# Loads held back by GpSimd reads, a first MLP step in halves, and list-scheduler ranks found by a search: windowed attention with a rational MLP on one core

## The chip, the cores and the metric

One core of a Trainium2 chip runs the whole program. The metric is the device time of one execution in microseconds. Before: 273.1 us, median of three runs (272.65 to 273.63).

Names used below: PE is TensorE's matmuls, PEld its weight loads, DVE VectorE, ACT ScalarE, POOL GpSimd, SP SyncE. A "filler" is a matmul of the identity whose result nobody reads.

## The reference, cut to what matters

```python
def _attn_ref(q, k, v, n_sink, window):          # B 4, H 8, S 768, D 64; n_sink 4, window 128
    scores = scale * np.matmul(q, k.transpose(0, 1, 3, 2))
    keep = is_sink | in_window                   # the first 4 keys, and the last 128
    scores = np.where(keep, scores, -1000000000.0)
    ...                                          # softmax over the kept keys
    return np.matmul(a, v).astype(np.float32)

def _moe_ref(x, w_in, w_out, a, b):              # 3072 tokens, 512 -> 2048 -> 512
    h = x @ w_in
    P = a[0] + a[1] * h + a[2] * h2 + a[3] * h3
    Q = 1.0 + np.abs(b[0]) * np.abs(h) + np.abs(b[1]) * h2
    g = P / (Q + 1e-06)
    return (g @ w_out).astype(np.float32)
```

The attention output of all heads, put side by side, is the x of the MLP.

## The kernel before

The 3072 tokens are cut into 12 steps of 256. A step loads K, Q and V (GpSimd, float32 to bf16), transposes K and Q (from step 3 on by DMA, from SyncE), computes scores, exponentials and the weighted sum, writes a normalized `x_n`, transposes it into `xblk` (two halves, by DMA from SyncE from step 3 on), and then runs the MLP: first products, the rational function on ScalarE and VectorE, second products, store. Attention runs some two steps ahead of the MLP.

The program is not written in order. Every piece of work is registered with an engine, an assumed length, a rank and the pieces it must follow:

```python
for s in range(NSTEP):
    r_ = 4 * s - 20
    ...
            piece(("load_k", s, t), "POOL", 0.9, r_, lambda s=s, t=t: load_k(s, t),
                  [("turned_k", s - 2)] if s > 2 else [], kind="sw", load=0.88)
    ...
    for h in range(H):
        piece(("load_v", s, h), "POOL", 0.62, r_ + 1.0, lambda s=s, h=h: load_v(s, h),
              [("attend", s - 2, 2)] if s >= 3 else [("ones", s)], kind="sw", load=0.32)
...
                piece(("turn_k", s, t), "SP", 1.25, 4 * s - 14, ...
                piece(("placed_x", s, grp), "SP", 1.25, r_, lambda s=s, grp=grp: turn_x_half(s, grp),
                      norms + [free], kind="hw", load=0.8)
```

A list scheduler then plays this through with the assumed lengths: whenever an engine is free it takes, among the pieces whose predecessors are done in the plan, the one of lowest rank (now and then it leaves the engine idle for a piece of much lower rank that is about to be ready). The order in which pieces are taken is the order of each engine's queue. Where TensorE has nothing to do in the plan, fillers are put in that are meant to keep its clock up:

```python
w = min(able, key=lambda w_: (w_.rank, w_.order))
...
if spin_from <= now and free["PE"] <= now + 1e-9:
    n = int((then - now) / 0.056)
    ...
    w.run = lambda n=n: spin(n)
```

Each queue runs in order, so a piece that waits holds up all behind it (the wait of 4.2 us in the table below is one).

The softmax here doesn't subtract the row's maximum and nothing guards it: scores larger than these inputs give would overflow.

## Time and profile before

| | before |
|---|---|
| median time | 273.1 us |
| span of the profiled execution | 270.1 us |
| busy: PE, DVE, ACT, POOL | 247.4, 230.3, 224.3, 121.3 us |
| fillers in the program | 395 |
| length of the kernel's own plan | 256.9 us |
| landing of a transpose of x, median: 60 to 130 us, 130 to 240 us | 6.4 us, 2.5 us |
| longest wait of PE for a transpose of x | 4.2 us |

PE's busy time contains the fillers, so it overstates useful work. The length of the plan is what the list scheduler's assumed lengths add up to; it is no chip time. The lines themselves are in the prediction, which shows them.

### The profile page before, as it was taken

Reading aid. Unit: us, or ns where it says so; the run is one execution under the profiler, and the core shown is the slowest. Engines: PE = TensorE matmul, PEld = TensorE weight load, DVE = VectorE, ACT = ScalarE, POOL = GpSimd, SP = SyncE. Lnnn points to the kernel's source line nnn. Section 1 sums busy time; section 2 is a strip of 40 time slices with the busy share of each in tenths; the row PEclk is TensorE's granted clock in tenths of the full one; section 3 lists DMA queues with packets and bytes.
Section 4 is the critical chain, followed back from the end, with each engine's and each line's share of the span. In section 5 each row is a group of like instructions: output and inputs, shape, how many; then the busy total and the mean of one; then the engine's idle time right before and its main releaser. Section 6 shows DMA issues by size and latency. Waiting matters only on the chain.

```text
span 270.1 us, 5649 instructions
## 1 busy us (share of the span) xinstructions
PE 247.4 (92%) x2294; PEld 188.8 (70%) x2315; DVE 230.3 (85%) x293; ACT 224.3 (83%) x216; POOL 121.3 (45%) x178
## 2 busy tenths in 40 slices
PE   5899878898989759998989999999999999999994
PEld 4789777885776449877767777867858776665442
DVE  7975289869996398999998999999989999999950
ACT  8643758499979828799999999999999999899831
POOL 8955889879697496683925013280000000000000
PEclk9999999999999979999999999999999999999999
DMA  7999999999999999999996344491030211110222
GB/s 196 99 153 194 68 102 121 175 136 158 136 164 149 121 195 207 134 130 164 148 138 97 34 70 58 31 103 46 19 101 9 69 41 58 45 55 0 81 78 78
DMA packets 109674, 28.07 MB, mean 104 GB/s; under 512 B 101456, under 2 KB 105552, under 8 KB 109648
## 3 DMA queue, kind: packets, MB, share of 16 engines
q0 software_dynamic: 74288, 12.99, 73.0%
q1 hardware_dynamic: 35360, 14.72, 28.3%
q8 instruction: 18, 0.29, 0.5%
q14 instruction: 8, 0.07, 0.1%
HBM read 27.30 MB, written 6.29 MB: 124 GB/s over the span
## 4 chain that ended last, share of the span: by engine, by line
PE 53%; DMA 21%; POOL 10%; ACT 8%; SPq 3%; issue 3%; DVE 1%; ACTq 0%; POOLq 0%
PE ps_out L613 22%; PE ps_h L516 21%; DMA w_in_sb<-in_moe_w_in_dram 7%; DMA qT<-q_bf 5%; PE ps_o L468 5%; DMA q_bf<-in_q_dram 4%; POOL w_out_sb L188 3%; PE ps_s L414 3%; POOL v_bd L179 2%; DMA w_out_sb<-in_moe_w_out_dram 2%; DMA xblk<-x_n 2%; PE ps_s L373 2%; POOL k_bf L171 2%; SPq L318 2%; ACT lnq L577 1%
## 5 line engine op out<-in xcount | busy, mean ns | idle before, releaser
L516 PE MATMUL ps_h<-xblk,w_in_sb 128*128 128x256 bf16 x768 | 91.6, 275 | 4.6 <-DMA xblk<-x_n 4.2
L613 PE MATMUL ps_out<-w_out_sb,g 128*128 128x512 bf16 x363 | 86.8, 379 | 1.8 <-ACT o_t L618 0.6
L516 PEld LDWEIGHTS <-w_in_sb 128*128 128x128 bf16 x768 | 75.0, 99 | 17.9 <-issue 4.4
L179 POOL DMA_DIRECT2D v_bd<-in_v_dram x96 | 63.4, 682 | 44.0 <-PE ps_o L468 28.0
L613 PEld LDWEIGHTS <-g 128*128 128x128 bf16 x384 | 36.6, 98 | 37.0 <-issue 0.9
L523 ACT ACTIVATE hb<-ps_h 128x1024 bf16<-128x1024 f32 x48 | 49.7, 1042 | 13.0 <-PE ps_h L516 12.8
L577 ACT ACTIVATE lnq<-den,one_eps,qsc 128x2048 f32<-128x2048 bf16 x24 | 50.6, 2114 | 1.7 <-DVE den L551 1.6
L583 ACT ACTIVATE den<-lnq 128x2048 bf16<-128x2048 f32 x24 | 46.5, 1938 | 0.0
L432 ACT ACTIVATE e<-ps_s 128x768 bf16<-128x768 f32 x48 | 39.8, 834 | 7.0 <-PE ps_s L420 4.5
L373 PE MATMUL ps_s<-ident 128*128 128x128 bf16 x395 | 30.1, 226 | 6.9 <-ACT e L432 5.4
L551 DVE TENSOR_TENSOR den<-den,sq 128x2048 bf16<-128x2048 bf16 x24 | 29.1, 1221 | 3.1 <-ACT sq L538 2.8
L373 PEld LDWEIGHTS <-ident 128*128 128x128 bf16 x395 | 25.7, 102 | 8.3 <-issue 5.7
L468 PE MATMUL ps_o<-v_bd,e 128*128 128x130 bf16 x352 | 28.5, 219 | 0.1
L589 DVE TENSOR_TENSOR g<-num,den 128x4096 bf16<-128x4096 bf16 (+1 forms) x13 | 27.6, 2123 | 0.6 <-ACT den L583 0.5
L571 DVE TENSOR_TENSOR num<-num,sq 128x4096 bf16<-128x4096 bf16 (+1 forms) x13 | 27.6, 2122 | 0.1
L567 DVE TENSOR_TENSOR sq<-sq,hb 128x4096 bf16<-128x4096 bf16 (+1 forms) x13 | 27.6, 2121 | 0.1
L538 ACT ACTIVATE sq<-hb 128x2048 bf16<-128x2048 bf16 x14 | 27.1, 1936 | 0.1
L468 PEld LDWEIGHTS <-e 128*128 128x128 bf16 x352 | 24.5, 97 | 2.8 <-ACT e L432 0.2
L414 PE MATMUL ps_s<-qT,kT 128*128 128x192 bf16 x192 | 23.8, 246 | 1.6 <-DMA qT<-q_bf 1.0
L618 ACT ACTIVATE o_t<-ps_out 128x512 f32<-128x512 f32 x24 | 14.5, 614 | 11.7 <-PE ps_out L613 8.1
L171 POOL DMA_DIRECT2D k_bf<-in_k_dram x22 | 20.9, 961 | 5.5 <-DMA kT_flat<-k_bf 4.6
L155 POOL DMA_DIRECT2D q_bf<-in_q_dram x21 | 20.5, 984 | 5.6 <-DMA qT<-q_bf 3.1
(84 smaller groups left out, 238.4 us busy)
## 6 DMA issues: line engine op xcount, KB each, us to landing
out_dram<-o_t SPq DMA_DIRECT2D x24, 256.0 KB, 3.1
v_bd<-in_v_dram POOLq DMA_DIRECT2D x96, 32.0 KB, 4.8
k_bf<-in_k_dram POOLq DMA_DIRECT2D x22, 128.0 KB, 6.3
q_bf<-in_q_dram POOLq DMA_DIRECT2D x21, 128.0 KB, 6.3
w_in_sb<-in_moe_w_in_dram POOLq DMA_DIRECT2D x8, 256.0 KB, 8.8
w_out_sb<-in_moe_w_out_dram POOLq DMA_DIRECT2D x16, 128.0 KB, 4.7
stage_q<-in_q_dram SPq DMA_DIRECT2D x1, 768.0 KB, 6.5
stage_kv<-in_k_dram SPq DMA_DIRECT2D x1, 512.0 KB, 4.3
```

The lines of the kernel that those rows point to most:

```text
L179: nc.gpsimd.dma_start(out=v_bd[s][e * 64:(e + 1) * 64, i, :, e, 0:D], in_=v[b, h, g * TS:(g + 1) * TS, :].rearrange("(j p) d -> p j d", p=64))
L373: nc.tensor.matmul(ps_scores[:, 0, 384:384 + P], lhsT=ident, rhs=ident, start=True, stop=True)
L414: nc.tensor.matmul(ps[:, n // 2, (n % 2) * 192:(n % 2) * 192 + 192], lhsT=kT_fix[s % 2][:, i * NHF + n, :], rhs=qT_fix[b % 2][:, i, c:c + ...
L432: nc.scalar.activation(out=data.rearrange("p (a n) c -> p a n c", a=2), in_=ps[:, :, 0:384].rearrange("p a (n c) -> p a n c", n=2), func=A ...
L468: nc.tensor.matmul(ps_o[:, u - u0, :], lhsT=l_, rhs=r_.rearrange("p e c -> p (e c)"), start=(m == 0), stop=(m == len(terms) - 1))
L516: nc.tensor.matmul(ps[:, n, :], lhsT=w_in_sb[c][:, fc * P:(fc + 1) * P], rhs=xblk[m][:, c, :], start=(c == 0), stop=(c == NDMC - 1))
L523: nc.scalar.activation(out=hb[m][:, j * GW:(j + 1) * GW], in_=ps_h.pop((m, j)).rearrange("p n c -> p (n c)"), func=AF.Copy)
L551: nc.vector.tensor_tensor(out=den[m][:, c], in0=den[m][:, c], in1=sq[m][:, c], op=ALU.add)
L567: nc.vector.tensor_tensor(out=sq[m][:, c], in0=sq[m][:, c], in1=hb[m][:, c], op=ALU.mult)
L577: nc.scalar.activation(out=lnq[m, part], in_=den[m][:, c], func=AF.Ln, scale=qsc, bias=one_eps)
L583: nc.scalar.activation(out=den[m][:, c], in_=lnq[m, part], func=AF.Exp, scale=-1.0)
L613: nc.tensor.matmul(ps_out[m, tt], lhsT=g_of[m][:, co:co + P], rhs=w_out_sb[fc], start=(fc == 0), stop=(fc == NFFC - 1))
```

## The change

Intent: the kernel before loads as early as buffers allow, so that its DMA traffic is crowded up to 140 us and thin afterwards. The change (a) holds loads back: a GpSimd copy of four elements reads `xblk` of step s, and the loads of K and Q of step s+3 and of V of step s+2 come after it in GpSimd's queue; (b) does the rational function of step 0 in two halves, as the last step already did; (c) lets the kernel, while it is built, move ranks of groups of pieces at random 2500 times and keep what shortens the plan, with some tolerance for worse plans at first. The new dependency of `sink_scores` in the diff is there to keep a searched order from a deadlock.

```diff
+    def touch_x(s):
+        nc.gpsimd.tensor_copy(out=scratch[0:1].rearrange("p (a b) -> p a b", a=2),
+                              in_=xblk[s][0:1, 0:NDMC:2, 0:TS:P])
...
+    LEAD = 3
+    for s in range(NSTEP - LEAD + 1):
+        piece(("touch", s), "POOL", 0.15, 4 * s - 9, lambda s=s: touch_x(s), [("turned_x", s)])
...
-                      [("turned_k", s - 2)] if s > 2 else [], kind="sw", load=0.88)
+                      [("turned_k", s - 2) if s > 2 else None,
+                       ("touch", s - LEAD) if s >= LEAD else None], kind="sw", load=0.88)
...                                     # the same for load_q; load_v after ("touch", s - LEAD + 1)
+        rv = r_ + 1.0 if s < LEAD - 1 else 4 * s - 16.4       # load_v's rank, was r_ + 1.0
...
-              [("spread_k", GPB * b)] + qts, takes="ps_m")
+              [("spread_k", GPB * b), ("attend", s - 2, 2) if s >= 2 else None] + qts,
+              takes="ps_m")
...
+    BY_HALF = (0, NSTEP - 1)
-        for hf, part in ((0, A_), (1, B_)) if last else ((None, None),):
+        by_half = m in BY_HALF
+        for hf, part in ((0, A_), (1, B_)) if by_half else ((None, None),):
...
+    def search(tries):
+        rnd = random.Random(1)
+        ...
+            ws, by = mates[rnd.choice(keys)], rnd.choice((-3, -2, -1, -0.5, 0.5, 1, 2, 3))
+            for w in ws:
+                w.rank += by
+            then = makespan(now + slack)
+            ...                         # keep it, or take it back
+    search(2500)
     for w in run_list():
```

The rest of the diff makes the list scheduler itself faster (heaps in place of list scans). With (a), (b) and (c) all taken out, the changed file builds the same instructions in the same order on every engine as the kernel before, with the dependency of `sink_scores` or without it.

More of the change, by code (lines that the diff above doesn't have):

```diff
@@ L2 @@
+import heapq
+import math
+import random
 from contextlib import ExitStack
@@ L506, in turn_x_half @@
             in_=x_n[s][:, 4 * grp * P:4 * (grp + 1) * P])
+    scratch = const_pool.tile([P, 4], BF16, name="scratch")
+    def touch_x(s):
+        nc.gpsimd.tensor_copy(out=scratch[0:1].rearrange("p (a b) -> p a b", a=2),
+                              in_=xblk[s][0:1, 0:NDMC:2, 0:TS:P])
     hb, sq, den, num, g_of, lnq, ps_h, ps_out, o_t = {}, {}, {}, {}, {}, {}, {}, {}, {}
@@ L663 @@
                 piece(("load_k", s, t), "POOL", 0.9, r_, lambda s=s, t=t: load_k(s, t),
-                      [("turned_k", s - 2)] if s > 2 else [], kind="sw", load=0.88)
+                      [("turned_k", s - 2) if s > 2 else None,
+                       ("touch", s - LEAD) if s >= LEAD else None], kind="sw", load=0.88)
             for n in range(2 * s + 1, min(2 * s + 3, NQT)):
                 piece(("load_q", n), "POOL", 0.9, r_ + 0.5, lambda n=n: load_q(n),
-                      [("turn_q", n - 4) if n - 4 >= NQ_HW else None], kind="sw", load=0.88)
+                      [("turn_q", n - 4) if n - 4 >= NQ_HW else None,
+                       ("touch", s - LEAD) if s >= LEAD else None], kind="sw", load=0.88)
         for h in range(H):
-            piece(("load_v", s, h), "POOL", 0.62, r_ + 1.0, lambda s=s, h=h: load_v(s, h),
-                  [("attend", s - 2, 2)] if s >= 3 else [("ones", s)], kind="sw", load=0.32)
+            piece(("load_v", s, h), "POOL", 0.62, rv, lambda s=s, h=h: load_v(s, h),
+                  [("attend", s - 2, 2) if s >= 3 else ("ones", s),
+                   ("touch", s - LEAD + 1) if s >= LEAD - 1 else None], kind="sw", load=0.32)
     for half in range(2):
@@ L856 @@
         last = m == NSTEP - 1
-        for hf, part in ((0, A_), (1, B_)) if last else ((None, None),):
-            w_ = HW if last else MW
+        by_half = m in BY_HALF
+        for hf, part in ((0, A_), (1, B_)) if by_half else ((None, None),):
+            w_ = HW if by_half else MW
             x_ = 0.0 if hf is None else 1.5 * hf
@@ L876 @@
                      [("turned_k", 0), ("turn_q3", 1)]))
+        if by_half:
+            for name in ("odd_h", "num", "gate"):
+                piece((name, m), "NONE", 0.0, 0, None, [(name, m, h_) for h_ in range(2)])
         for tt in range(NTS):
@@ L884 @@
                       lambda m=m, tt=tt, f0=f0, f1=f1: project_out(m, tt, f0, f1),
-                      [("gate", m, part) if last else ("gate", m)]
+                      [("gate", m, part) if by_half else ("gate", m)]
                       + [("load_w_out", c) for c in range(f0, f1)]
@@ L898, with run_list @@
     HOLD_R, HOLD_F = 3.0, 0.5
-    def run_list():
+    follow = {}
+    for w in work.values():
+        w.names = list(dict.fromkeys(w.after))
+        for a_ in w.names:
+            follow.setdefault(a_, []).append(w)
+    def run_list(limit=None):
         gap = {"PE": 0.18, "DVE": 0.13, "ACT": 0.15, "POOL": 0.1, "SP": 0.1, "NONE": 0.0}
@@ L904, in run_list @@
         waiting = {e: [] for e in engines}
-        follow, left = {}, {}
+        left = {}
         for w in work.values():
-            names = set(w.after)
-            left[w.name] = len(names)
-            for a_ in names:
-                follow.setdefault(work[a_].name, []).append(w)
-            if not names:
+            left[w.name] = len(w.names)
+            if not w.names:
                 waiting[w.eng].append(w)
@@ L921, in run_list @@
         returns = []
+        times = sorted(f_ for f_ in free.values() if f_)
         while len(done) < len(work) + len(spun):
-            for end, w in [x_ for x_ in ends if x_[0] <= now + 1e-9]:
-                ends.remove((end, w))
+            if limit is not None and now > limit:
+                return None
+            while ends and ends[0][0] <= now + 1e-9:
+                w = heapq.heappop(ends)[2]
                 for f_ in follow.get(w.name, ()):
@@ L928, in run_list @@
                         waiting[f_.eng].append(f_)
-            for end, p_ in [x_ for x_ in returns if x_[0] <= now + 1e-9]:
-                returns.remove((end, p_))
-                room[p_] += 1
+            while returns and returns[0][0] <= now + 1e-9:
+                room[heapq.heappop(returns)[1]] += 1
             moved = False
             for e in engines:
-                if free[e] > now + 1e-9:
+                if free[e] > now + 1e-9 or not waiting[e]:
                     continue
-                able = [w for w in waiting[e]
-                        if (not w.takes or room[w.takes])
-                        and (not w.kind or lanes[w.kind][count[w.kind] % 8] <= now + 1e-9)]
-                if not able:
+                best, w = None, None
+                for w_ in waiting[e]:
+                    if ((best is None or (w_.rank, w_.order) < best)
+                            and (not w_.takes or room[w_.takes])
+                            and (not w_.kind
+                                 or lanes[w_.kind][count[w_.kind] % 8] <= now + 1e-9)):
+                        best, w = (w_.rank, w_.order), w_
+                if w is None:
                     continue
-                w = min(able, key=lambda w_: (w_.rank, w_.order))
                 if any(f_.eng == e and left[f_.name] == 1 and f_.rank < w.rank - HOLD_R
-                       for end, x_ in ends if end < now + HOLD_F * w.length
+                       for end, _, x_ in ends if end < now + HOLD_F * w.length
                        for f_ in follow.get(x_.name, ())):
@@ L961, in run_list @@
                     lanes[w.kind][count[w.kind] % 8] = end
+                    heapq.heappush(times, end)
                     count[w.kind] += 1
@@ L965, in run_list @@
                 if w.frees:
-                    returns.append((end, w.frees))
-                ends.append((end, w))
+                    heapq.heappush(returns, (end, w.frees))
+                heapq.heappush(ends, (end, w.order, w))
+                heapq.heappush(times, free[e])
+                heapq.heappush(times, end)
                 done.append(w)
             if not moved:
-                times = ([f_ for f_ in free.values() if f_ > now + 1e-9] + [x_[0] for x_ in ends]
-                         + [x_[0] for x_ in returns]
-                         + [x_ for l_ in lanes.values() for x_ in l_ if x_ > now + 1e-9])
-                then = min(x_ for x_ in times if x_ > now + 1e-9)
-                if spin_from <= now and free["PE"] <= now + 1e-9:
+                while times and times[0] <= now + 1e-9:
+                    heapq.heappop(times)
+                if not times:
+                    return None
+                then = times[0]
+                if limit is None and spin_from <= now and free["PE"] <= now + 1e-9:
                     n = int((then - now) / 0.056)
@@ L984, in run_list, with makespan @@
         return done
+    def makespan(limit):
+        done = run_list(limit)
+        return 1e9 if done is None else max(w.start + w.length for w in done if w.run)
+    def search(tries):
+        rnd = random.Random(1)
+        mates = {}
+        for name, w in work.items():
+            mates.setdefault(name[:2], []).append(w)
+        keys = sorted((key for key, ws in mates.items() if ws[0].run), key=str)
+        best = now = makespan(1e8)
+        kept = {w.name: w.rank for w in work.values()}
+        for n in range(tries):
+            heat = 0.25 * (1 - n / tries) + 0.01
+            slack = -heat * math.log(1 - rnd.random())
+            ws, by = mates[rnd.choice(keys)], rnd.choice((-3, -2, -1, -0.5, 0.5, 1, 2, 3))
+            for w in ws:
+                w.rank += by
+            then = makespan(now + slack)
+            if then <= now + slack:
+                now = then
+                if now < best:
+                    best = now
+                    kept = {w.name: w.rank for w in work.values()}
+            else:
+                for w in ws:
+                    w.rank -= by
+        for w in work.values():
+            w.rank = kept[w.name]
+    search(2500)
     for w in run_list():
```

## The prediction

> **What bounds the kernel now.** I read the busy shares and 40 slices first, then the engines' busy time by stage, then the timelines of TensorE, VectorE and SyncE around the worst stretch.
>
> ```profile
> PE 247.4 (92%) x2294; PEld 188.8 (70%) x2315; DVE 230.3 (85%) x293; ACT 224.3 (83%) x216; POOL 121.3 (45%) x178
> ...
> PEclk9999999999999979999999999999999999999999
> DMA  7999999999999999999996344491030211110222
> ```
>
> Three engines are near balance, so no single one is "the" bound. The DMA row says when transfers are crowded: up to about slice 21 (some 140 us), then hardly at all. The one dip of the TensorE clock is in the crowded part.
>
> ```profile
> 19.00:50.10 31.10, 27.10 (x369) 24.81 (x367) 19.78 (x25) 18.63 (x19) 24.63 (x35) 1.00 1.32 127
> 50.10:69.00 18.90, 17.67 (x172) 13.88 (x171) 15.84 (x20) 15.80 (x17) 16.43 (x24) 1.00 1.83 154
> 69.00:97.28 28.28, 22.86 (x205) 17.03 (x206) 21.02 (x30) 22.89 (x23) 20.68 (x27) 0.99 2.07 148
> 97.28:120.00 22.72, 22.67 (x204) 18.64 (x205) 21.65 (x27) 17.40 (x17) 17.65 (x24) 0.93 2.22 170
> ...
> 140.00:240.00 100.00, 99.18 (x836) 72.68 (x847) 96.20 (x105) 98.09 (x87) 15.35 (x24) 1.00 0.32 58
> ```
>
> The columns after the length are PE, PEld, DVE, ACT, POOL busy, clock, DMA share, GB/s. From 140 to 240 us PE, DVE and ACT are at 99, 96 and 98 of 100: that stretch cannot shrink much, since the change removes no arithmetic. What can shrink lies before 120 us: from 19 to 120 us ACT idles 12.5 + 3.1 + 5.4 + 5.3 = 26.3 us and DVE 11.3 + 3.1 + 7.3 + 1.1 = 22.8 us. PE looks busy there, but part of it is filler: matmuls of the identity that only keep the clock up, 164 of them (11.1 us busy) between 19 and 50 us.
>
> The worst single loss is at 93 us:
>
> ```profile
> 92.67 0.38 PE L516 MATMUL ps_h<-xblk,w_in_sb 128*128 128x256 bf16 x2
> 97.28 2.93 PE L516 MATMUL ps_h<-xblk,w_in_sb 128*128 128x256 bf16 x13 [4.23 <-DMA xblk<-x_n]
> ```
>
> TensorE begins step 3's first MLP product and stops 4.23 us for the second half of step 3's transposed attention output. Why is that half late? VectorE wrote its last piece from 81.69 to about 82.2 us. SyncE's queue:
>
> ```profile
> 82.60 1.28 SPq L504 DMA_TRANSPOSE xblk<-x_n x1
> 83.97 2.58 SPq L335 DMA_TRANSPOSE kT_flat<-k_bf x2
> 86.65 4.23 SPq L318 DMA_TRANSPOSE qT<-q_bf x2
> 90.97 1.22 SPq L504 DMA_TRANSPOSE xblk<-x_n x1
> ```
>
> The missing half stands at 90.97, behind four transposes of K and Q. Counting transposes from the start (K of step 3 is the first, Q tiles start with number 6) these four belong to step 6. They could get ahead only because the loads had run three steps ahead of x. Then the transfer itself took 6.27 us in the chain of waits (90.97 to 97.24). So an operand ready at 82.2 us arrived 15 us later.
>
> **What the Trainium skill says.**
> - "DMA: Bandwidth & Descriptors", section "Issuing engines are not separate DMA queues": transfers issued from sync, scalar and GpSimd all run on the same 16 DMA engines and interleave. The trace agrees: the transposes of x took a median of 6.4 us to land between 60 and 130 us (DMA crowded), and 2.5 us between 130 and 240 us.
> - "TensorE: Matmul & The Clock Gate", section "What's actually happening": after an idle window of about 3.4 us the array goes to half clock. The trace agrees: after the 4.23 us wait the granted clock reads 0.50 over 97 to 100 us, and the 62 matmuls up to 105.67 us took 8.39 us where 16 take 1.75 us elsewhere (62 would take 6.8): 1.6 us more.
> - "Perfetto Trace Analysis", section "DMA Instruction — SWDGE (GPSIMD)": the instruction's end on GpSimd is the end of writing descriptors, not of the data. The trace agrees: a load of V occupies GpSimd 0.68 us and lands a median of 4.8 us after issue. So GpSimd's 45% does not say how far the loads are; only the waits of their readers do.
> - "VectorE: DVE Perf Modes", section "The TRN2 errata — SBUF-src ops pay a fixed extra latency per instruction": halving an operation pays it twice. The trace agrees, with small numbers (below).
>
> **The change, part by part.**
>
> *1. The hold.* Ten GpSimd copies of four elements read the transposed x of step s; the loads of K and Q of step s+3 and of V of step s+2 come after them. Each copy costs GpSimd what its small operations cost in this trace, 0.1 to 0.3 us: under 3 us over the run on an engine busy 45%, off the path. The effect is in order: K and Q of step 6 cannot be loaded before x of step 3 has landed, so the four transposes quoted above cannot stand before it. SyncE then issues the half at about 83.9 us, when its first half has been issued, not at 90.97: 7 us earlier. Even at an unimproved 6.3 us to landing it is there at 90.2, before TensorE asks at 92.67. The wait (4.2 us) and the half clock (1.6 us) go: 5.8 us on TensorE, with ACT idle 5.3 us in the 23 us after it because it waited on those products, so both are on the path. I book 5.0, as the next waiter may be ready only a little earlier. A second place of the same kind: at 120.6 to 125.5 us TensorE runs 48 fillers (2.7 us at 56 ns each) and waits 1.5 us while a Q transpose issued at 114.55 takes 7.36 us; ACT is 96% busy there, so I book only 1.0.
>
> *2. Step 0's MLP by halves.* Now VectorE stands still before this line:
>
> ```profile
> 34.05 0.20 DVE L479 RECIPROCAL rec<-ps_o 128x6 f32<-128x6 f32 x1 [5.61 <-PE ps_o L468]
> ...
> 41.32 1.46 DVE L557 TENSOR_SCALAR num<-sq,acoef 128x4096 bf16<-128x4096 bf16 x1
> ```
>
> Step 0's first half has its denominator at 28.45 us; the full-width numerator waits for the second half, whose weights came late, until 41.3. By halves, the first four operations (0.7 + 0.7 + 1.14 + 1.14 = 3.7 us by start-to-start times of the last step's halves) fit into the 5.6 us of idle time. Price, from the rows by shape: a half product takes 1.22 us and starts 1.14 after the one before, a full one 2.29 and 2.20: +0.07 us for each of three, about +0.08 for each of two others, 0.4 us in all. So some 3.3 us of VectorE work leaves the stretch from 41 to 53 us. There the chain of waits runs through GpSimd issue and loads of output weights, K and Q, not VectorE, so most of it is hidden; I book 1.2 net.
>
> *3. The ranks found by search.* It adds no instruction; it reorders all queues for the kernel's own model of itself. Ideal room: the 22.8 us of DVE idle before 120 us, less the 7.3 + 1.1 that part 1 attacks, is 14.4, of which about half is the wait for weights at the head (9 us for each of the two waves of input weights in the chain). From the remaining 7 I book a quarter, 1.8: the old ranks were tuned already, and the model's landing times are fixed while the trace's run from 2.4 to 8.3 us.
>
> *New cost.* Held loads come closer to their use. From the landing of x(s) to K and Q of s+3 ready: four issues of 0.9 us, 6.3 to landing, four transposes of 1.25 us on SyncE and about 6 to landing: 3.6 + 6.3 + 5 + 6 = 21 us at present durations, against about 18 us for a step. Attention runs some two steps ahead of the MLP, so this is mostly slack; I subtract 0.5.
>
> Sum: 5.0 + 1.0 + 1.2 + 1.8 - 0.5 = 8.5 us; 273.1 - 8.5 = 264.6, say 264.5 us.
>
> **The rivals.**
> - *The held load becomes the wait.* For it: the 21 us above, and each queue is in order, so a score placed too early by the model stalls TensorE. Against: fewer transfers at once should bring landing times down, as they do after 130 us. If it bites in each of the nine later steps with 1 us, the gain is eaten: 272 to 275 us.
> - *The later part gets slower.* Loads that now end at 181 us will end later, beside the transposes of x that now take 2.5 us. For it: 6.4 us when crowded. Against: 1.6 MB of Q, K and V a step at some 150 GB/s is 10.5 us of 18, and each hold opens just after an x has landed. It would take 2 to 3 us: 267 us.
> - *The hand-tuned order was better on the chip than the searched one*, as a model's optimum leaves no slack: near 270 us.
> - *The search does better than I book*: if most of the 22.8 us idle before 120 goes, 256 us. ACT and DVE at 96 to 98% afterwards bound it there.
>
> **Range and chances.** Centre 264.5; a good search with the hold reaches 257, a hold that bites 271. "Faster by over 2%" needs under 267.6, a gain of 5.5: the hold alone nearly gives it, and any two parts do. Chances: faster 0.72, within 2% 0.23, slower 0.05.
>
> **What would show it.** Right: no wait of over 1 us of the first product for x; the clock at 1.00 after 20 us; K and Q transposes of step s+3 behind x(s) on SyncE; x landing in 3 to 5 us before 130 us; GpSimd loads stretched to about 200 us with waits for the transposed x; half-width operations near 28 to 34 us; ACT and DVE idle before 120 us down by 8 us or so; the stretch of full load unchanged in pace. Wrong: TensorE waiting on Q or K transposes or V loads in each step, or more fillers after 60 us; then the hold is too tight. If the gain lies before 60 us, the search did it and not the hold.

## The result, and the profile after

| | before | after |
|---|---|---|
| median, same rounds | 272.88 us (4 runs) | 265.47 us (4 runs, 265.06 to 267.09) |
| ratio, 95% interval | | 0.974, 0.969 to 0.979 |
| span of the profiled execution | 270.1 us | 264.1 us |
| fillers | 395 | 328 |
| length of the plan | 256.9 us | 252.2 us |
| x landing, median, 60 to 130 us | 6.4 us | 3.4 us |

Ratios here and below are the mean time of one kernel's fast runs over that of the other's fast runs of the same rounds, so not quite the ratio of the medians beside them.

The page of the changed kernel, its first line and the clock and DMA rows of the 40 slices:

```profile
PE 245.7 (93%) x2248; PEld 185.3 (70%) x2248; DVE 231.9 (88%) x298; ACT 223.4 (85%) x216; POOL 129.5 (49%) x188
...
PEclk9799999999999999999999999999999999999999
DMA  6999799999995599968986999959770413021122
```

The crowded part of the DMA row now has gaps in it and reaches to slice 30 (198 us). The dip of the clock in mid-run is gone; one at the start is new.

Busy time by stage of the changed kernel, the same stages and columns as in the prediction (PE, PEld, DVE, ACT, POOL, clock, DMA share, GB/s):

```profile
19.00:50.10 31.10, 27.43 (x350) 24.99 (x348) 24.22 (x35) 19.57 (x21) 24.80 (x38) 1.00 1.35 127
50.10:69.00 18.90, 16.75 (x175) 13.66 (x174) 11.89 (x18) 15.34 (x16) 15.06 (x22) 1.00 1.77 140
69.00:97.28 28.28, 26.42 (x246) 19.44 (x245) 27.53 (x34) 23.25 (x24) 17.30 (x23) 1.00 1.07 120
97.28:120.00 22.72, 22.25 (x214) 18.01 (x212) 19.72 (x25) 22.45 (x22) 12.23 (x16) 1.00 1.30 119
...
140.00:240.00 100.00, 98.83 (x830) 71.89 (x829) 99.12 (x103) 97.32 (x87) 35.97 (x47) 1.00 0.73 86
```

ACT's idle time from 19 to 120 us is now 11.5 + 3.6 + 5.0 + 0.3 = 20.4 us, 5.9 less than before; DVE's is 6.9 + 7.0 + 0.8 + 3.0 = 17.7, 5.1 less. Nearly all of ACT's part is in the last of these stages, the one after the wait at 93 us. That is about the size of the 6.0 us by which the span is shorter.

SyncE's queue of the changed kernel at the same place (start, us, operation):

```profile
82.68 2.50 SPq L507 DMA_TRANSPOSE xblk<-x_n x2
85.28 5.32 SPq L632 DMA_DIRECT2D out_dram<-o_t x2
93.46 3.90 SPq L507 DMA_TRANSPOSE xblk<-x_n x2
97.45 2.63 SPq L338 DMA_TRANSPOSE kT_flat<-k_bf x2
```

Both halves of step 3's x now go out together at 82.68 us, and K of step 6 comes at 97.45. VectorE's timeline at the head:

```profile
28.39 0.81 DVE L567 TENSOR_SCALAR num<-sq,acoef 128x2048 bf16<-128x2048 bf16 x1
29.24 0.81 DVE L572 TENSOR_SCALAR sq<-sq,acoef 128x2048 bf16<-128x2048 bf16 x1
30.08 1.23 DVE L577 TENSOR_TENSOR sq<-sq,hb 128x2048 bf16<-128x2048 bf16 x1
31.34 1.22 DVE L581 TENSOR_TENSOR num<-num,sq 128x2048 bf16<-128x2048 bf16 x1
```

The first half's four operations fill what was idle time. GpSimd's longest wait in the changed kernel is the one that was built in (total, times, longest):

```profile
POOL scratch L515 <- DMA xblk<-x_n: 53.0, 7, 11.0
```

So far everything looks as predicted, and the time is within 1 us of it. The next section takes the parts one by one, and the picture changes.

### The profile page after: what moved, and what is told of

The parts are those of the page before. It is cut to its first block, busy times and chain, and to the rows that moved or that the text cites. A ratio compares the mean times of both kernels' runs of the same rounds, so it can differ in the third digit from the quotient of the medians.

```text
span 264.1 us, 5572 instructions
## 1 busy us (share of the span) xinstructions
PE 245.7 (93%) x2248; PEld 185.3 (70%) x2248; DVE 231.9 (88%) x298; ACT 223.4 (85%) x216; POOL 129.5 (49%) x188
## 3 DMA queue, kind: packets, MB, share of 16 engines
q0 software_dynamic: 74288, 12.99, 67.8%
## 4 chain that ended last, share of the span: by engine, by line
PE 48%; DVE 21%; ACT 12%; DMA 9%; issue 4%; POOL 4%; ACTq 0%; DVEq 0%
PE ps_out L623 22%; PE ps_h L526 15%; PE ps_o L471 5%; DMA kT_flat<-k_bf 4%; ACT hb L533 4%; DMA w_in_sb<-in_moe_w_in_dram 3%; PE ps_s L417 3%; DVE den L561 3%; ACT lnq L587 3%; DVE x_n L484 3%; PE ps_s L376 2%; ACT e L435 2%; DVE den L556 2%; ACT den L593 2%; DVE g L599 2%
## 5 line engine op out<-in xcount | busy, mean ns | idle before, releaser
L526 PE MATMUL ps_h<-xblk,w_in_sb 128*128 128x256 bf16 x768 | 90.6, 273 | 0.2 <-ACT xblk L504 0.2
L623 PE MATMUL ps_out<-w_out_sb,g 128*128 128x512 bf16 x384 | 89.5, 379 | 0.5 <-ACT o_t L628 0.5
L526 PEld LDWEIGHTS <-w_in_sb 128*128 128x128 bf16 x768 | 74.2, 98 | 11.4 <-DMA v_bd<-in_v_dram 0.7
L515 POOL COPY scratch<-xblk 1x4 bf16<-1x4 bf16 x10 | 9.1, 914 | 55.6 <-DMA xblk<-x_n 53.0
L376 PE MATMUL ps_s<-ident 128*128 128x128 bf16 x328 | 26.7, 232 | 6.9 <-ACT e L435 5.1
L376 PEld LDWEIGHTS <-ident 128*128 128x128 bf16 x328 | 22.8, 105 | 9.0 <-issue 6.0
L158 POOL DMA_DIRECT2D q_bf<-in_q_dram x21 | 22.0, 1064 | 0.4 <-issue 0.4
L484 DVE SCALAR_TENSOR_TENSOR x_n<-ps_o,csc,rec 128x384 bf16<-128x384 f32 (+1 forms) x36 | 20.6, 573 | 1.3
```

Source lines behind the costliest of these rows:

```text
L376: nc.tensor.matmul(ps_scores[:, 0, 384:384 + P], lhsT=ident, rhs=ident, start=True, stop=True)
L526: nc.tensor.matmul(ps[:, n, :], lhsT=w_in_sb[c][:, fc * P:(fc + 1) * P], rhs=xblk[m][:, c, :], start=(c == 0), stop=(c == NDMC - 1))
L623: nc.tensor.matmul(ps_out[m, tt], lhsT=g_of[m][:, co:co + P], rhs=w_out_sb[fc], start=(fc == 0), stop=(fc == NFFC - 1))
```

## The experiments

Twelve kernels ran in three jobs, on the chip together with the kernel before each time. All gave correct results. "Theory" numbers in the expectations stand for: 1, the hold is the main term, as predicted; 2, the search made the gain and the hold costs; 3, the parts need each other; 3', in runs 5 to 7, the hold pays only under ranks searched for it.

### The parts alone (runs 1 to 3)

Run 1, the hold alone: the changed kernel with

```diff
-    BY_HALF = (0, NSTEP - 1)
+    BY_HALF = (NSTEP - 1,)
-    search(2500)
```

> The kernel before with the hold alone: the ten copies, the loads behind them, V's later rank; no halves of step 0, no search. Theory 1 (the hold is the main term, as predicted, 6 of the 8.5 us): ratio 0.975 to 0.985, no wait of TensorE for x of step 3, clock 1.00 from 20 us on. Theory 2 (the search made the gain, the hold costs: the kernel's own model of itself puts this one 4.7 us longer than the kernel before, 261.6 against 256.9): ratio 1.01 to 1.02. Theory 3 (the parts need each other): about 1.00 here and for the search alone.

Measured: 274.86 us against 273.51, ratio 1.009 (0.999 to 1.019). Not faster, on a chip whose runs of before spread from 270.4 to 275.7. Yet the mechanism did what was predicted: the trace lists no wait of PE for x (it lists those over 0.15 us), and x landed in 3.3 us (median, 60 to 130 us). Three things in its trace can have taken the gain back; none was tested alone. First, a new wait, seen in PE's timeline of this run:

```profile
64.04 0.48 PE L417 MATMUL ps_s<-qT,kT 128*128 128x192 bf16 x2 [2.40 <-DMA qT<-q_bf]
64.32 0.63 PE L384 MATMUL ps_sink<-qT,k_sink 128*128 128x128 bf16 x4
64.74 3.02 PE L623 MATMUL ps_out<-w_out_sb,g 128*128 128x512 bf16 x8
```

Scores wait 2.40 us for a transposed Q, and the eight products after them take 3.02 us where eight took 1.89 elsewhere in the same trace: the half clock again, only at another place (the granted clock is 0.62 over 64.7 to 67.8 us). Second, fillers. The group of fillers, in the kernel before and in this run (count, busy us and mean ns, idle before):

```profile
L373 PE MATMUL ps_s<-ident 128*128 128x128 bf16 x395 | 30.1, 226 | 6.9 <-ACT e L432 5.4 <-POOL ident masks.py:199 1.4
```

```profile
L376 PE MATMUL ps_s<-ident 128*128 128x128 bf16 x475 | 36.4, 230 | 7.5 <-ACT e L435 5.9 <-POOL ident masks.py:199 1.4
```

80 fillers more at 56 ns each are 4.5 us more in which the plan had nothing for PE: with the hand-set ranks the plan itself is 4.7 us longer (261.6 us). Third, the stretch of full load became looser:

```profile
140.00:240.00 100.00, 98.70 (x844) 72.72 (x855) 94.25 (x104) 94.31 (x84) 35.32 (x47) 1.00 0.75 91
```

DVE and ACT at 94 of 100 us, where the kernel before had 96.2 and 98.1.

Run 2, the halves alone: the changed kernel without touch pieces and their dependencies, V's rank back at `r_ + 1.0`, and no `search(2500)`.

> The kernel before with step 0's MLP by halves alone. Theory 1: 1.2 us net at best, ratio 0.993 to 1.000. Rival (the head was bound by VectorE after all): 0.985 or less. The kernel's own model puts it 0.4 us shorter.

Measured: 270.25 us, ratio 0.993 (0.983 to 1.003), 1.9 us in the mean. In the expected range; not distinguishable from nothing with three rounds.

Run 3, the search alone: without touch pieces, `BY_HALF = (NSTEP - 1,)`.

> The kernel before with the search alone (with the dependency of the sink scores that keeps a searched order from a deadlock); no hold, no halves. Theory 1: about 2 us, ratio 0.985 to 0.997, and step 3's x still late behind K and Q of a later step or crowded. Theory 2 (the search made the gain; the kernel's own model puts this one 6.8 us shorter than before): ratio 0.970 to 0.980. Theory 3: about 1.00.

Measured: 269.08 us, ratio 0.9815 (0.968 to 0.995), 5.0 us in the mean. The interval excludes 1 and reaches into both theories' ranges. x is as late as before (5.8 us to land).

### The same plan, with and without the real wait (run 4)

```diff
-        piece(("touch", s), "POOL", 0.15, 4 * s - 9, lambda s=s: touch_x(s), [("turned_x", s)])
+        piece(("touch", s), "POOL", 0.15, 4 * s - 9, lambda s=s: None, [("turned_x", s)])
```

The plan and all queue orders stay those of the changed kernel; only the ten copies are missing, so GpSimd no longer waits for x.

> The changed kernel with the ten copies left out of the program but kept in the list scheduler's plan: the order of every queue is the same (compared instruction by instruction), only GpSimd no longer waits for x. Theory A (what counts is the order of SyncE's queue, which the plan alone sets): 0.970 to 0.980, as the changed kernel, or a little less. Theory B (what counts is that the loads really stay off the DMA engines until x has landed): x lands in 5 to 6 us again between 60 and 130 us and the ratio is 0.985 to 1.00.

Measured: 269.08 us, ratio 0.987 (0.978 to 0.997), where the changed kernel has 0.974. x lands in 4.9 us (expected 5 to 6, just missed; the changed kernel 3.4). The stage from 69 to 97 us, the changed kernel first, then this run:

```profile
69.00:97.00 28.00, 26.14 (x245) 19.28 (x244) 27.25 (x34) 22.97 (x24) 17.30 (x23) 1.00 1.06 120
```

```profile
69.00:97.00 28.00, 23.84 (x213) 16.77 (x214) 25.11 (x30) 22.47 (x22) 20.38 (x29) 1.00 1.88 144
```

Same orders, but a DMA share of 1.88 in place of 1.06 and 2.1 us less of DVE's work done. VectorE's timeline shows where: it waits 2.46 us for the transposed K up to 84.68 us and 2.00 us up to 128.09 us, two waits that the changed kernel does not have. So within this plan the real hold is worth 0.9874 - 0.974 = 1.3%, some 3.6 us, and crowded transfers are what the traces show in its absence (theory B). The two ratios come from different jobs and their intervals overlap slightly.

### The parts in pairs (runs 5 to 7)

Run 5: the changed kernel with `BY_HALF = (NSTEP - 1,)`.

> The changed kernel without the halves of step 0. Theory 3' (the hold pays only under ranks searched for it, the halves are worth little): ratio 0.970 to 0.982, within a percent of the changed kernel's 0.974. Rival (the halves carry the gain that the hold and the search do not): 0.985 or more. The kernel's own model: 251.6, the changed kernel 252.2.

Measured: 271.01 us, ratio 0.995 (0.989 to 1.000). The rival's range, and a surprise. PE waits 4.6 us for transposed Q in two places, and two slices of the clock row read 7.

Run 6: the changed kernel without touch pieces and their dependencies, V's rank back.

> The changed kernel without the hold. Theory 3': as the search alone (0.9815) or as the plan without copies (0.987), so 0.978 to 0.990, with x landing in 5 to 6 us between 60 and 130 us. Rival (the hold brings nothing once the ranks are searched): 0.970 to 0.976. The kernel's own model: 251.5.

Measured: 265.66 us, ratio 0.976 (0.971 to 0.982). That equals the changed kernel within noise, without any hold. The landing of x between 60 and 130 us is the slowest of all:

```profile
DMA to landing us min/median/max: 6.5/6.8/6.9
```

And yet PE waits for x only 1.0 us in the whole run, and step 3's first products start at 92.76 us and run through. Counted as in the prediction, SyncE issues the second half of step 3's x at 85.94 us here, behind two transposes of K of step 5 and ahead of those of K of step 6 (87.56 us). The search alone had found the order that the hold was built to enforce. ACT's idle time from 19 to 120 us is 20.2 us, the same as in the changed kernel.

Run 7: the changed kernel without `search(2500)`.

> The changed kernel without the search: hand ranks. Theory 3' (hand ranks were made for a kernel without the hold, and its plan has more filler with it; the model puts this one 1.5 us longer than before): 1.00 to 1.01. Rival (search only adds a little to the two others): 0.98 to 0.985.

Measured: 272.82 us, ratio 1.004 (0.999 to 1.010), as theory 3' has it.

### The order of SyncE's queue alone (run 8)

```diff
-        piece(("turn_q", n), "SP", 1.25, 4 * s - 14, lambda n=n: turn_q(n), [("load_q", n), last],
+        piece(("turn_q", n), "SP", 1.25, 4 * s - 14, lambda n=n: turn_q(n), [("load_q", n), last, ("turned_x", s - 3) if s >= 3 else None],
-                      [("load_k", s, t), if_step(s - 3, "spread_k") if s - 3 >= NS_PE else None],
+                      [("load_k", s, t), if_step(s - 3, "spread_k") if s - 3 >= NS_PE else None,
+                       ("turned_x", s - 3)],
```

made in the kernel before. The scheduler then plans all queues anew, so pieces on other engines move too. It tests the core of the prediction's first part: that the wait at 93 us is made by four transposes standing in front.

> The kernel before with one thing changed in its plan: the transposes of K and Q of step s+3 stand in SyncE's queue behind those of x of step s; the loads still run ahead as before, no copies, no halves, no search. If the order of SyncE's queue alone made the wait of 4.2 us: that wait and the half clock go, 0.980 to 0.985. If crowding of the DMA engines counts as much: x still lands in 5 to 7 us, and 0.99 to 1.00. The kernel's own model: 257.6, before 256.9.

Measured: 272.46 us, ratio 1.002 (0.997 to 1.007). SyncE and PE of this run:

```profile
82.54 1.25 SPq L507 DMA_TRANSPOSE xblk<-x_n x1
...
84.52 1.21 SPq L507 DMA_TRANSPOSE xblk<-x_n x1
```

```profile
92.02 3.43 PE L526 MATMUL ps_h<-xblk,w_in_sb 128*128 128x256 bf16 x30 [0.25 <-DMA xblk<-x_n]
```

The half goes out at 84.52 in place of 90.97, and PE's wait is 0.25 us in place of 4.23, although x still takes 6.1 us to land. The cause of the wait is thereby shown. But the run is no faster: the wait went as the first theory said, the time did not. The half clock did not go either. It moved to a place some 20 us earlier, behind two waits for a transposed Q:

```profile
75.36 0.33 PE L417 MATMUL ps_s<-qT,kT 128*128 128x192 bf16 x2 [1.62 <-DMA qT<-q_bf]
77.01 0.47 PE L417 MATMUL ps_s<-qT,kT 128*128 128x192 bf16 x2 [1.33 <-DMA qT<-q_bf]
77.28 3.15 PE L526 MATMUL ps_h<-xblk,w_in_sb 128*128 128x256 bf16 x16
```

The sixteen products take 3.15 us where sixteen took 1.91 later in this trace, and the granted clock is 0.50 from 77 to 79 us. In all, PE waits 3.2 us for Q here, 1.0 us in the kernel before. The stretch of full load:

```profile
140.00:240.00 100.00, 97.92 (x852) 73.31 (x866) 95.05 (x101) 95.29 (x85) 19.89 (x27) 1.00 0.43 68
```

ACT does 2.8 us less in these 100 us than before. The milestones below, counted from the timelines, show the gain and its loss (each column is one profiled execution; that of run 8 was the fastest of its six).

| end of | before | hold alone | order alone | changed |
|---|---|---|---|---|
| x_n of step 3 (DVE) | 82.2 | 85.6 | 84.1 | 83.0 |
| first products of step 3 copied (ACT) | 107.0 | 104.5 | 102.1 | 105.7 |
| x_n of step 6 | 140.1 | 140.1 | 134.1 | 131.7 |
| first products of step 7 copied | 180.5 | 182.1 | 176.2 | 172.8 |
| first products of step 11 copied | 246.6 | 250.6 | 245.7 | 243.7 |
| span | 270.1 | 273.5 | 269.2 | 264.1 |

Order alone is 4.9 us ahead at step 3, 6.0 at step 6, 4.3 at step 7 and 0.9 at step 11. The fillers suggest why: from 120 to 140 us there are 69 before and 16 here, but from 140 to 240 us 29 before and 76 here. The idle time that the old plan had put early stands later in the new one. The 47 fillers more are 2.6 us at 56 ns each, and 3.4 us of the lead are lost between step 7 and step 11. That the one makes the other fits, but was not tested.

### Other draws of the search (runs 9 to 12)

The search cells so far are one random sequence each. Runs 9 and 10 are the changed kernel, 11 and 12 the kernel of run 6, with

```diff
-        rnd = random.Random(1)
+        rnd = random.Random(2)          # and 3
```

> The changed kernel with another start of the search's random numbers (2 instead of 1); the kernel's own model puts it at 252.5, the changed kernel at 252.2. Theory Q (hold, halves and search together make the gain, whatever order the search happens on): 0.969 to 0.979. Theory P (the search draws a plan, and plans that the model holds equal differ on the chip by a per cent or two): anything from 0.97 to 0.995.

> As the run before with start 3; the model puts it at 250.3, 1.9 us under the changed kernel. Theory Q: 0.969 to 0.979. Theory P: 0.97 to 0.995. If the model's differences between searched plans count on the chip, this is the fastest of all, 0.967.

> Halves and search without the hold, start 2; the model puts it at 251.5, as start 1 (which measured 0.976). If the hold is worth something under a search: 0.98 or more. If it is worth nothing: the mean of this, the next and the start-1 run lies within half a per cent of the mean of the three with the hold.

> Halves and search without the hold, start 3; the model puts it at 251.7. Read with the run before: the mean of the three starts without the hold against the mean of the three with it.

Measured, with the length of each plan beside it:

| | start 1 | start 2 | start 3 | mean |
|---|---|---|---|---|
| hold, halves, search: ratio | 0.974 | 0.972 (0.967 to 0.976) | 0.986 (0.982 to 0.990) | 0.977 |
| its plan, us | 252.2 | 252.5 | 250.3 | |
| halves, search: ratio | 0.976 | 0.990 (0.986 to 0.994) | 0.981 (0.977 to 0.985) | 0.982 |
| its plan, us | 251.5 | 251.5 | 251.7 | |

Theory P, the draw of a plan, has it: the intervals of starts 2 and 3 do not touch in either row. The shortest plan of the upper row is its slowest kernel; the three lower plans are within 0.2 us of each other and their times within 1.4%. What a bad draw looks like on the chip, in the waits of PE of run 10 (total, times, longest):

```profile
PE ps_s L417 <- DMA qT<-q_bf: 4.2, 2, 3.5
PE ps_h L526 <- DMA w_in_sb<-in_moe_w_in_dram: 2.0, 2, 1.7
```

These are waits for transfers, whose landing the plan assumes too early. In the changed kernel neither row exists. But such waits do not tell a bad draw from a good one: run 9, the fastest by its ratio, waits 2.9 us for a transposed Q, and run 11, the slowest without the hold, not at all. Nor does the clock alone: its row shows a slice of 8 or less in mid-run in runs 9, 10 and 11, none in run 12 and the changed kernel. What makes a draw good stays open. The difference of the row means, 0.005, is as large as its standard error from this spread (0.006, from the two rows' standard deviations of 0.0076 and 0.0070 over three draws each). So whether the hold pays under a search is not settled.

Run 9 has the lowest ratio of all, but its interval covers the changed kernel's ratio; no version was shown to be faster than the changed kernel.

### All cells together

| | no search | search (start 1) |
|---|---|---|
| nothing | 1.000 (plan 256.9) | 0.9815 (250.1) |
| halves | 0.993 (256.5) | 0.976 (251.5) |
| hold | 1.009 (261.6) | 0.995 (251.6) |
| hold and halves | 1.004 (258.4) | 0.974 (252.2) |

Adding the search multiplies the time by 0.9815, 0.983, 0.986 and 0.970 in the four rows: always down, 2.0% or 5.5 us in the mean. Adding the halves gives 0.993, 0.995, 0.996 and 0.979: 0.9%, 2.5 us, of which most is one cell. Adding the hold gives 1.009, 1.013, 1.011 and 0.998: 0.8% or 2 us slower. These are point estimates: the searched cells are one draw each, and draws differ by some 0.7%. With the means of three starts in place of start 1, the search gives 0.989 in the row of the halves and 0.973 in that of hold and halves; its poorest draw (run 11, 0.990) is not separable from the halves with hand ranks (0.993).

Among the five kernels with hand-set ranks the length of the plan puts the times in order: 256.5, 256.9, 257.6 (run 8), 258.4 and 261.6 us, with ratios 0.993, 1.000, 1.002, 1.004 and 1.009, though neighbours are not separable. That runs 1 and 8 won nothing is thus what their own plans said. Among searched plans the length says nothing of the kind, and run 5 (251.6 us, 0.995) is no faster than the halves with hand ranks.

## Why the prediction was right or wrong

The time was right: 264.5 predicted, 265.47 measured. The sum that led to it was not: one term was too large and another too small by about the same amount, so the agreement of the total is luck.

**What bounds the kernel: right.** The stretch of full load did not shrink, and the gain came from before 120 us, where ACT lost 5.9 us of idle time and DVE 5.1. I had said 8 "or so".

**The hold's mechanism: right, its worth: wrong.** That four transposes of step 6 before step 3's x made the wait is shown by run 8, which moved them behind it. That crowding stretches x's landing is shown by run 4. The clock went with the wait in the changed kernel. The step that failed is "the wait (4.2 us) and the half clock (1.6 us) go: 5.8 us on TensorE [...] so both are on the path": I concluded it from ACT's idle time just after the wait. Run 8 took 4 us of that wait away and won nothing (1.002): step 3's products were done 4.9 us earlier, and by step 11 0.9 us of that was left. What the step left out is that the order which removes the wait comes with a new plan. That plan is 0.7 us longer (257.6) and has more fillers after 140 us, and under it PE waits 2.2 us more for Q and still meets a half clock. Run 6 shows the other side: there the wait goes without any hold, by the search's order. Booked 6.0 us for the hold; alone it measured about 2.4 us slower (ratio 1.009 of 273, interval from nothing to 5 us slower), within one fixed plan 3.6 us faster, and over three draws of the search 1.4 us faster with an error of the same size. My sign for telling the two apart ("if the gain lies before 60 us, the search did it and not the hold") failed too: ACT's busy time from 19 to 60 us is 26.0 us before and after, and from 60 to 120 us it rises from 48.7 to 54.6 us, but without the hold, in run 6, it rises to 52.6 us as well.

**The halves: right in place, undersized perhaps.** The four operations run from 28.39 to 32.56 us as worked out. Booked 1.2 us net; alone 1.9 us, without being separable from zero; averaged over the cells 2.5 us.

**The search: undersized.** Booked 1.8 us as "a quarter" of the room; measured 5.0 us alone and 5.5 in the mean of four cells. The argument for a small number, that the old ranks were tuned already, was wrong: they left a plan of 256.9 us where the search finds 250 to 252. The other argument, that the plan's landing times are not the chip's, stands: the spread of 1.4% among equal plans fits it.

**The cost of the hold.** I subtracted 0.5 us for loads that come later. In the changed kernel (start 1 of the search) the trace lists no wait of PE for Q or K, so the rival "the held load becomes the wait" did not bite TensorE there (VectorE waits 4.8 us for a transposed K, 4.4 us before). It did in runs 5, 9 and 10 (4.6, 2.9 and 4.2 us for Q); run 3, which has no hold, waits for Q too, so the hold is not its only cause. The copies took 9.1 us of GpSimd in all, not under 3; GpSimd's share rose from 45 to 49% and no wait for a copy appears in the trace. I had taken 0.1 to 0.3 us from GpSimd's small operations at the start of the kernel; the ten copies took 0.19 to 2.07 us. The longest, first VectorE, then GpSimd:

```profile
153.20 2.29 DVE L581 TENSOR_TENSOR num<-num,sq 128x4096 bf16<-128x4096 bf16 x1
```

```profile
153.46 2.07 POOL L515 COPY scratch<-xblk 1x4 bf16<-1x4 bf16 x1 [2.63 <-DMA xblk<-x_n]
```

The one ends at 155.49 us, the other at 155.53. So it is with all ten: each ends 0.03 to 0.04 us after an operation of VectorE that had begun before it. The Trainium skill, "GPSIMD Engine Reference", section "1. Specifications", says that GpSimd's SBUF interfaces are shared with VectorE, with contention when a VectorE instruction has two SBUF inputs or runs in a 2-port mode. These ends agree with it; no experiment tested the cause.

**The other rivals.** "The later part gets slower" did not come: DVE even rose to 99.1 of 100 us, and x lands in 2.7 us (median) from 130 to 240 us. Loads end at 196.7 us, as said (about 200). "Hand-tuned order was better than the searched one" has all four pairs of cells against it.

**What stays open:** whether the hold pays at all when the search is drawn often; why the draw of run 5 is so much worse than its plan says, beyond its waits for Q and the clock dips that follow; which of the search's many moves matter; and whether the later fillers are what took run 8's lead.

## What to carry to other kernels

In a statically scheduled kernel the longest wait can go and the time stay, because the order that removes it moves other work as well: look at what the new plan does behind that place. Change the plan and the mechanism together, and measure each with the other fixed (here, the same queue orders with and without the ten copies). A search over the kernel's own model was worth about 2% here, but its last per cent is a lottery: draw several plans, time them on the chip, and do not credit a companion change with what a lucky draw brought. And a total that agrees with the prediction proves no term of its sum.

## What the Trainium skill lacked or had wrong

- "DMA: Bandwidth & Descriptors", section "DMA Transpose (X-bar)", has constraints and alternatives, but no time to landing for a small transpose within SBUF, issued while other transfers run. Here one of 128 partitions by 512 columns of bf16 occupies SyncE's queue for 1.19 us at least, and lands in 2.4 us at best, in 6.8 us (median of run 6, 60 to 130 us) when loads crowd the engines.
- No page that I read says what becomes of time won at one place of a statically scheduled program; runs 1 and 8 are two cases where nothing came of it (ratios 1.009 and 1.002 with the wait of 4.2 us gone).
